# Taking GpSimd out of a weight conversion, norms off ScalarE, and a list schedule with other durations: windowed attention with a cosine-gated MLP on one core

## The chip, the cores and the metric

One core of a Trainium2 chip runs the kernel. The metric is the device time of one execution in microseconds (us). Engines are named as in the profile: PE is TensorE, DVE is VectorE, ACT is ScalarE, POOL is GpSimd, and SP is SyncE, which here only issues DMAs.

## The reference

```python
def _attn_ref(q, k, v, n_global, n_local):      # q, k, v: 4 x 8 x 768 x 64
    scores = scale * np.matmul(q, k.transpose(0, 1, 3, 2))
    ...                                          # is_global: the first 8 keys; is_local: the last 96
    scores = np.where(keep, scores + bias[None], -1000000000.0)
    a = np.exp(scores - np.max(scores, axis=-1, keepdims=True))
    a = a / (np.sum(a, axis=-1, keepdims=True) + 1e-09)
    return np.matmul(a, v).astype(np.float32)

def _moe_ref(x, w_in, w_out):                    # x: 3072 x 512, d_ff: 2048
    h = x @ w_in
    g = h * np.cos(h)
    return (g @ w_out).astype(np.float32)
```

The attention's output, 3072 tokens by 512, is the x of the second part. All numbers are 32-bit floats.

## The kernel before

The 3072 tokens are eight **chunks** of 384. A chunk has four head **pairs**, which gives 32 attention units. A unit's scores come from PE (L521 for the first eight units, L525 after), DVE folds and reduces them (L538, L547), ACT takes the exponentials (L572), DVE adds and inverts the sums (L580, L583), a **norm** multiplies the exponentials by the inverse, PE transposes them (L669), DVE masks them into `pv` (L677, L682), and PE multiplies by v (L704). The result is split into a high part `xh` and a rest `xl` (L725). Splitting every operand of a product into a rounded high part and a rest, and multiplying three times, is how 32-bit accuracy is kept.

The norm can run on three engines: one DVE instruction (L605, or two of L600 in a batch's first chunk), one or two POOL instructions of the same line, or four ACT instructions (L596).

The second part runs in 128 **steps**, one for each chunk and each of 16 slices f of d_ff. A step has 12 matmuls of 384 columns (L740, four quarters of three, one quarter for each pair of the chunk), then a chain over ACT and DVE (`turns` L757, `angle` L760, `cosine` L763, product L798, copy `gh`, difference `gl` L807), then 9 matmuls of 512 columns (L751). The steps are taken in phases: chunk 0 with slices 0 to 7, chunk 1 with all 16, chunk 0 with 8 to 15, then chunk by chunk. Steps are counted here from 0 in this order.

Weights arrive as 64-bit words and each of the 32 slices (`wi` and `wo`, 512 KB each) is **converted** on the chip by six instructions: `wlow` (L378 on ACT, L380 elsewhere), `wsign` (L385 on DVE, L388 on POOL), `wbias` (L394 on ACT, L396), `wjoin` (L399, DVE alone), `whigh` (L253 ACT, L255 DVE, L257 POOL) and `wrest` (L409).

A planner in the kernel decides the order. Each operation names its engines with a duration in ns on each, and what it must follow; `Plan.run` places them on a list schedule, earliest due first, and picks an engine by cost. The program is emitted in that order, so every engine runs its queue strictly in order. An operation with `port=True` is never planned at the same time on DVE as an instruction of POOL:

```python
                held = self.port > t
                holds = lambda o, x: x == POOL or (x == DVE and o.port)
...
                        if held and holds(o, e):
                            continue
```

`EARLY` spaces the due times of the four pairs of chunks 0 and 1. Where PE is planned to be idle in the first 45 us of the plan, filler matmuls on zeros (L1044) are emitted.

Of the kernel before, what the change touches and what calls it, by code (L numbers as in the profile page):

```python
# [27 lines left out]
SLOT = R + G  # L28
# [15 lines left out]
PERIOD = 5200  # L44
LAG = 3.5
MARGIN, EACH = 3.2, 3.2
EARLY = {0: 2500, 1: 7500}
WEIGHT = {PE: 1, ACT: 0.5, DVE: 1.2, POOL: 0.8}

PHASES = [(0, 0, 8), (1, 0, 16), (0, 8, 16)]  # L50
# [182 lines left out]
class Net:  # L233
# [124 lines left out]
    def plan_weights(self, f):  # L358


        nc, p = self.nc, self.plan
        cols = self.w_in.bitcast(U32)[f]
        rows = self.w_out.bitcast(U32)[f * P : (f + 1) * P, :]
        ends = []
        for kind, src, out in (("wi", cols, self.wi), ("wo", rows, self.wo)):
            raw = self.const.tile([P, 512, 2], U32, name="raw", tag=f"{kind}{f}")
            w0, w1 = raw[:, :, 0], raw[:, :, 1]
            wu = Slot("wu", lambda i: self.work.tile([P, 512], U32, name="wu", tag=i))
            box = {}

            def dma(e, raw=raw, src=src):
                nc.sync.dma_start(raw.rearrange("p c w -> p (c w)"), src)


            def wlow(e, raw=raw, w0=w0):
                h = raw.bitcast(I32)[:, :, 0]
                if e == ACT:
                    nc.scalar.activation(h, w0, AF.Copy, scale=7.49 * 2.0**-32)  # L378
                else:
                    self.eng(e).tensor_scalar(h, w0, 7.49 * 2.0**-32, 1.0, op0=ALU.mult, op1=ALU.mult)  # L380

            def wsign(e, raw=raw):
                if e == DVE:
                    h = raw.bitcast(U16)
                    nc.vector.tensor_scalar(h[:, :, 1], h[:, :, 3], 0x8000, None, op0=ALU.bitwise_and)  # L385
                else:
                    h = raw.bitcast(BF16)
                    nc.gpsimd.tensor_scalar(h[:, :, 1], h[:, :, 3], 0.0, 1.0, op0=ALU.mult, op1=ALU.mult)  # L388

            def wbias(e, w1=w1):  # L390

                x = w1.bitcast(F32)
                if e == ACT:
                    nc.scalar.activation(x, x, AF.Copy, scale=2.0**-112)  # L394
                else:
                    self.eng(e).tensor_scalar(x, x, 2.0**-112, 1.0, op0=ALU.mult, op1=ALU.mult)  # L396

            def wjoin(e, w0=w0, w1=w1, wu=wu):
                nc.vector.scalar_tensor_tensor(  # L399
                    wu.tile, w1, 3, w0, op0=ALU.logical_shift_left, op1=ALU.bitwise_or  # L400
                )

            def whigh(e, kind=kind, out=out, wu=wu, box=box):
                out[f] = box["w"] = self.const.tile([P, 2, 512], F32R, name="w", tag=f"{kind}{f}")
                self.copy(e, box["w"][:, 0, :], wu.tile.bitcast(F32))

            def wrest(e, wu=wu, box=box):
                w = box["w"]
                self.eng(e).tensor_tensor(  # L409
                    w[:, 1, :], wu.tile.bitcast(F32), w.bitcast(F32)[:, 0, :], op=ALU.subtract  # L410
                )

            o = p.op({SP: 470}, dma, extra=1460)
            o = p.op({ACT: 620, DVE: 400, POOL: 700}, wlow, [o], port=True)
            o = p.op({DVE: 610, POOL: 1310}, wsign, [o], port=True)
            o = p.op({ACT: 575, DVE: 345, POOL: 655}, wbias, [o], port=True)
            o = p.op({DVE: 605}, wjoin, [o], [wu], port=True)
            o = p.op({ACT: 525, DVE: 335, POOL: 595}, whigh, [o], [wu], port=True)
            ends.append(p.op({DVE: 605, POOL: 1245}, wrest, [o], [wu], port=True))
        return ends  # L420


# [41 lines left out]
    def plan_unit(self, L, pr):  # L464
# [13 lines left out]
        if exact:  # L478
            raw = row()
            src = self.qk[b, c, 2 * pr : 2 * pr + 2]  # L480

            def load(e):
                nc.sync.dma_start(raw.tile[:, k0:], src.rearrange("j p w -> (j p) w")[:, k0:])

            def queries(e):
                x = raw.tile[:, KW:]
                if e == ACT:
                    nc.scalar.activation(x, x, AF.Copy, scale=self.steep[:, pr : pr + 1])
                else:
                    self.eng(e).tensor_scalar(x, x, self.steep[:, pr : pr + 1], 1.0, op0=ALU.mult, op1=ALU.mult)  # L490

            o = p.op({SP: 470}, load, [], [raw], extra=1422 * (QK - k0) // 1000)
            ready = [p.op({ACT: 430, DVE: 270, POOL: 470}, queries, [o], [raw], port=True)]
            heads = [(raw, ready)] * 2
        else:
            heads = [self.plan_split(row(), self.qk[b, c, 2 * pr + j], k0, self.steepness(2 * pr + j)) for j in range(2)]
# [10 lines left out]
        for js, h in [(js, h) for js in (((0, 1),) if exact else ((0,), (1,))) for h in range(0, CT, 2)]:  # L507
# [17 lines left out]
                            nc.tensor.matmul(out, qs[:, m, q0], ks[:, k : k + w], start=m == 0, stop=m == 1)  # L525

            cols = sum(part(t)[1] for t in ts)
            cost = cols * 17 // 10 if exact else cols * 2 * 46 // 100
            so = self.chain("s", p.op(
                {PE: cost}, score, [o for j in js for o in heads[j][1]],  # L530
                list(pss.values()) + [heads[j][0] for j in js[:1]] + [st, tt[h // 2]], mode="rows" if exact else None,
# [1 line left out]
            for j, ps in pss.items():  # L533
                i0 = 1 if lead(h) else 0

                def fold(e, ps=ps, i0=i0):
                    w = ps.tile[:R, i0 * WIN : 2 * WIN].rearrange("p (a w) -> p a w", w=WIN)
                    nc.vector.copy_predicated(w[:, :, :R], self.mine.bitcast(U32)[:, i0:], w[:, :, SLOT:])  # L538

                o = p.op({DVE: 60 + 100 * (2 - i0)}, fold, [so], [ps])  # L540
                for i, t in enumerate(ts):

                    def least(e, i=i, t=t, j=j, ps=ps):
                        w = width(t)
# [37 lines left out]
        def rec(e):  # L582
            nc.vector.reciprocal(st.tile[:, 2 * n2 :], st.tile[:, n2 : 2 * n2])  # L583

        o = p.op({DVE: 70}, add, exps, [st])
        o = p.op({DVE: 120}, rec, [o], [st])
        u["norm"] = []
        for h in range(0, CT, 2):

            def norm(e, h=h):  # L590
                x = tt[h // 2].tile.rearrange("p t j w -> p (t j) w")
                r = st.tile[:, 2 * n2 + 2 * h : 2 * n2 + 2 * h + 4].rearrange("p (c o) -> p c o", o=1)
                if e == ACT:
                    for i in range(4):
                        w = width(h + i // 2)
                        nc.scalar.activation(x[:, i, :w], x[:, i, :w], AF.Copy, scale=r[:, i])  # L596
                    return
                if lead(h):
                    for a, w in ((0, R), (2, SLOT)):
                        self.eng(e).tensor_tensor(  # L600
                            x[:, a : a + 2, :w], x[:, a : a + 2, :w],
                            r[:, a : a + 2].broadcast_to([R, 2, w]), op=ALU.mult,
                        )
                    return
                self.eng(e).tensor_tensor(x, x, r.broadcast_to([R, 4, SLOT]), op=ALU.mult)  # L605

            u["norm"].append(
                p.op({DVE: 70 + 2 * 2 * SLOT * 104 // 100, ACT: 560, POOL: 100 + 4 * SLOT * 22 // 10}, norm, [o], [tt[h // 2], st], port=True)
            )
        return u  # L610

    def plan_split(self, raw, src, k0, sc):
# [27 lines left out]

        loads = [p.op({SP: 470}, lambda e, a=a: load(e, a), [], [raw], extra=711 * (QK - k0) // 1000) for a in (0, D)]
        w = KW - k0
        q = self.chain("qhigh", p.op({ACT: 370}, qhigh, loads, [raw, qk]))
        q = p.op({DVE: 470}, qrest, [q], [raw, qk], port=True)
        k = self.chain("khigh", p.op(
            {ACT: 50 + w * 427 // 512, DVE: 70 + w * 265 // 512, POOL: 100 + w * 490 // 512},
# [118 lines left out]
    def plan_step(self, s, n, f, a, b):  # L765
# [10 lines left out]
        for kk in range(self.NK):  # L776

            def m1(e, kk=kk):
                self.moe1(ph.tile, *x.tile, f, kk)

            done = self.chain(f"m1 {s}", p.op(
                {PE: 522}, m1, [self.xdone[n, kk], self.wdone[f][0]], [ph, x], due=due + (kk + 1) * 522,
            ))
            if kk == 0:
                self.chain("m1", done)
# [3 lines left out]
        for c0, c1 in pieces:  # L789
# [20 lines left out]
            for t in range(c0 // P, c1 // P):  # L810

                def m2(e, t=t):
                    self.moe2(po[t].tile, *gg.tile, f, t, f == a, f == b)

                o = self.chain("m2", p.op(
                    {PE: 697}, m2, [g, self.wdone[f][1]], [po[t], gg], due=due + int(LAG * PERIOD) + (t + 1) * 697,
                ))
                if f == b:
                    self.plan_store(n, t, po[t], o, b < self.NF - 1, due + int((LAG + 1) * PERIOD))
# [284 lines left out]
```

## Time and profile before

| what | value |
|---|---|
| median of 3 runs | 723.63 us (722.34 to 723.75) |
| the profiled execution's own time | 723.99 us |
| its span | 722.3 us |
| mean granted TensorE clock | 0.981 of full |
| PE, PEld busy | 697.8 us (97%), 603.4 us (84%) |
| DVE, ACT, POOL busy | 509.9 us (71%), 489.4 us (68%), 129.1 us (18%) |
| DMA | 55.75 MB, mean 77 GB/s |

Busy time is the time in which an engine had at least one instruction running; in a matmul row the modelled end is included, so neighbours overlap. 1.7 us of the execution's time lie outside the span. "Idle before" in a row is the idle time of that engine just ahead of the instruction, and the name behind the arrow is what ended it.

### The profile page before, as it was taken

How to read it: one execution, taken by the hardware profiler on the slowest of the kernel's cores; microseconds unless marked ns; L12 is line 12 of the kernel's file. 1: busy time of each engine (PE TensorE's matmuls, PEld its weight loads, DVE VectorE, ACT ScalarE, POOL GpSimd, SP SyncE). 2: the span in 40 equal slices, each digit the busy share in tenths (PEclk: the TensorE clock that was granted, in tenths of full speed). 3: DMA queues.
4: the chain of work that ended last, by engine and by line, in shares of the span. 5: the costliest groups of instructions: out<-in, count | busy, mean ns of one | idle time of the engine just before them, and what ended most of it. 6: DMA issues, size and time to landing. Idle time of an engine off the chain costs nothing.

```text
span 722.3 us, 13066 instructions
## 1 busy us (share of the span) xinstructions
PE 697.8 (97%) x4481; PEld 603.4 (84%) x4481; DVE 509.9 (71%) x1505; ACT 489.4 (68%) x1267; POOL 129.1 (18%) x170
## 2 busy tenths in 40 slices
PE   7977989999999999999999999999999999999996
PEld 4646768988899888888889888898888888989984
DVE  7898988886875887567774778757775778644332
ACT  7888987677775667577773886657775796644332
POOL 6345445630000211110000121101000120100000
PEclk8897999999999999999999999999999999999998
DMA  8997121022330322213121322203222210001001
GB/s 304 404 351 194 35 58 35 1 57 64 81 96 1 110 61 57 57 51 96 52 61 40 110 61 57 58 0 101 64 67 66 81 56 1 1 1 44 0 1 49
DMA packets 32605, 55.75 MB, mean 77 GB/s; under 512 B 3473, under 2 KB 18193, under 8 KB 32529
## 3 DMA queue, kind: packets, MB, share of 16 engines
q1 hardware_dynamic: 32528, 54.82, 25.4%
q8 instruction: 37, 0.61, 0.4%
q14 instruction: 40, 0.32, 0.1%
HBM read 48.52 MB, written 6.29 MB: 76 GB/s over the span
## 4 chain that ended last, share of the span: by engine, by line
PE 81%; DVE 7%; ACT 5%; issue 1%; DMA 0%; ACTq 0%; DVEq 0%
PE bank L740 34%; PE bank L751 34%; PE bank L704 5%; PE bank L525 5%; PE bank L669 3%; DVE wu L399 2%; DVE w L409 1%; ACT w L253 1%; ACT rr L763 1%; ACT raw L394 1%; DVE gl L807 1%; DVE tt L547 1%; ACT tt L596 1%; DVE bank L538 1%; DVE raw L385 1%
## 5 line engine op out<-in xcount | busy, mean ns | idle before, releaser
L740 PE MATMUL bank<-xh,w 128*128 128x384 f32 x1024 | 297.9, 343 | 4.4 <-DVE rr L798 3.2
L751 PE MATMUL bank<-w,gh 128*128 128x512 f32 x768 | 244.0, 399 | 0.0
L740 PEld LDWEIGHTS bank<-xh,w 128*128 128x128 f32 x1024 | 190.0, 190 | 12.0 <-DVE rr L798 3.6
L740 PE MATMUL bank<-xl,w 128*128 128x384 f32 x512 | 173.8, 339 | 2.7 <-DVE xl L725 2.7
L751 PEld LDWEIGHTS bank<-w,gh 128*128 128x128 f32 x768 | 138.9, 189 | 21.4 <-issue 0.3
L751 PE MATMUL bank<-w,gl 128*128 128x512 f32 x384 | 152.5, 397 | 0.0
L760 DVE SCALAR_TENSOR_TENSOR rr<-rr,bank 128x384 f32<-128x384 int32 x129 | 69.8, 543 | 104.4 <-ACT rr L757 104.3
L757 ACT ACTIVATE rr<-bank 128x384 int32<-128x384 f32 x129 | 62.0, 482 | 118.2 <-PE bank L740 117.8
L763 ACT ACTIVATE rr<-rr,half_pi 128x384 f32<-128x384 f32 x129 | 78.9, 614 | 43.9 <-DVE rr L760 42.7
L798 DVE TENSOR_TENSOR rr<-bank,rr 128x384 f32<-128x384 f32 x129 | 71.0, 552 | 46.7 <-ACT rr L763 45.9
L740 PEld LDWEIGHTS bank<-xl,w 128*128 128x128 f32 x512 | 97.3, 190 | 7.5 <-DVE xl L725 3.3
L572 ACT ACTIVATE tt<-tt,st 96x104 f32<-96x104 f32 (+1 forms) x256 | 94.4, 370 | 9.7 <-DVE st L547 8.2
L751 PEld LDWEIGHTS bank<-w,gl 128*128 128x128 f32 x384 | 72.4, 189 | 16.8
L257 POOL TENSOR_SCALAR ks<-raw 128x408 fp32r<-128x408 f32 (+1 forms) x43 | 24.7, 574 | 301.6 <-PE bank L525 284.3
L807 DVE TENSOR_TENSOR gl<-rr,gh 128x384 fp32r<-128x384 f32 (+1 forms) x115 | 66.7, 580 | 7.7 <-ACT gh L253 5.7
L547 DVE CUSTOM_DVE_ANT_0 tt<-bank,dd 96x104 f32<-96x104 f32 (+1 forms) x256 | 55.5, 257 | 3.0
L253 ACT CAST gh<-rr 128x384 fp32r<-128x384 f32 (+1 forms) x92 | 46.5, 507 | 11.3 <-DVE rr L798 4.6
L704 PEld LDWEIGHTS bank<-pv,v 104*64 104x64 f32 (+1 forms) x960 | 42.7, 140 | 12.8 <-issue 7.1
L596 ACT ACTIVATE tt<-tt,st 96x104 f32<-96x104 f32 (+1 forms) x152 | 44.6, 369 | 8.4 <-DVE st L583 8.1
L525 PEld LDWEIGHTS bank<-ks,qs 128*96 128x96 f32 x384 | 45.9, 162 | 4.7 <-issue 0.3
L704 PE MATMUL bank<-pv,v 104*64 104x96 f32 (+1 forms) x960 | 48.8, 254 | 0.6 <-ACT pv L253 0.6
L538 DVE COPY_PREDICATED bank<-mine,bank 96x192 f32<-96x192 uint32 (+1 forms) x128 | 40.6, 330 | 11.1 <-PE bank L525 8.0
(97 smaller groups left out, 766.5 us busy)
## 6 DMA issues: line engine op xcount, KB each, us to landing
raw<-in_qk_dram SPq DMA_DIRECT2D x48, 224.0 KB
raw<-in_qk_dram SPq DMA_DIRECT2D x48, 198.0 KB
raw<-in_w_in_dram SPq DMA_DIRECT2D x16, 512.0 KB
raw<-in_w_out_dram SPq DMA_DIRECT2D x16, 512.0 KB
out_dram<-oo SPq DMA_DIRECT2D x24, 256.0 KB
v<-in_v_dram SPq DMA_DIRECT2D x16, 240.0 KB
v<-in_v_dram SPq DMA_DIRECT2D x16, 192.0 KB
raw<-in_qk_dram SPq DMA_DIRECT2D x4, 448.0 KB
```

Of the source, the lines that this page charges most:

```text
L253: self.nc.scalar.copy(out, x)
L525: nc.tensor.matmul(out, qs[:, m, q0], ks[:, k : k + w], start=m == 0, stop=m == 1)
L547: nc.vector.tensor_tensor_reduce(tt[t // 2].tile[:, t % 2, j, :w], ps.tile[:R, i * WIN : i * WIN + w], self.dd[:, v, :w], op0=ALU.add, op1 ...
L572: nc.scalar.activation(x, x, AF.Exp, bias=st.tile[:, c : c + 1], scale=-1.0, accum_out=st.tile[:, n2 + c : n2 + c + 1])
L704: nc.tensor.matmul(px.tile[j * D : (j + 1) * D, t * R : (t + 1) * R], vs.tile[:k, t + c, hs][:, j * D : (j + 1) * D], pv[:k, c, o : o + R] ...
L740: self.nc.tensor.matmul(ph[:, :CW], self.wi[f][:, w, kk * P : (kk + 1) * P], xx[:, kk, :], start=kk == 0 and m == 0, stop=kk == self.NK - ...
L751: self.nc.tensor.matmul(po, gg[:, ts], self.wo[f][:, w, :], start=start and m == 0, stop=stop and m == 2)
L757: self.nc.scalar.activation(r.bitcast(I32), ph, AF.Copy, scale=1.0 / TWO_PI, bias=0.25)
L760: self.nc.vector.scalar_tensor_tensor(r, r.bitcast(I32), -TWO_PI, ph, op0=ALU.mult, op1=ALU.add)
L763: self.nc.scalar.activation(r, r, AF.Sin, bias=self.half_pi)
L798: {DVE: dve}, lambda e, r=r, h=h: nc.vector.tensor_tensor(r(), h(), r(), op=ALU.mult), [o], [ph, rr]
L807: self.eng(e).tensor_tensor(g[1][:, cs], r(), g[0].bitcast(F32)[:, cs], op=ALU.subtract)
```

## The change

The conversion's six operations lose their POOL durations, so that POOL has no part in it; the norm loses its ACT form; and a number of planned durations, the due spacing `EARLY`, and some `port` flags are other numbers. No arithmetic is added. The code that emits an instruction is the same apart from the norm's ACT branch.

```diff
-EARLY = {0: 2500, 1: 7500}
+EARLY = {0: 3000, 1: 6000}
...
             o = p.op({SP: 470}, dma, extra=1460)
-            o = p.op({ACT: 620, DVE: 400, POOL: 700}, wlow, [o], port=True)
-            o = p.op({DVE: 610, POOL: 1310}, wsign, [o], port=True)
-            o = p.op({ACT: 575, DVE: 345, POOL: 655}, wbias, [o], port=True)
-            o = p.op({DVE: 605}, wjoin, [o], [wu], port=True)
-            o = p.op({ACT: 525, DVE: 335, POOL: 595}, whigh, [o], [wu], port=True)
-            ends.append(p.op({DVE: 605, POOL: 1245}, wrest, [o], [wu], port=True))
+            o = p.op({ACT: 580, DVE: 500}, wlow, [o], port=True)
+            o = p.op({DVE: 650}, wsign, [o], port=True)
+            o = p.op({ACT: 580, DVE: 345}, wbias, [o], port=True)
+            o = p.op({DVE: 600}, wjoin, [o], [wu], port=True)
+            o = p.op({ACT: 525, DVE: 335}, whigh, [o], [wu], port=True)
+            ends.append(p.op({DVE: 600}, wrest, [o], [wu], port=True))
...
-            ready = [p.op({ACT: 430, DVE: 270, POOL: 470}, queries, [o], [raw], port=True)]
+            ready = [p.op({ACT: 520, DVE: 300, POOL: 490}, queries, [o], [raw], port=True)]
...
-        self.chain("worst", p.op({DVE: 75}, worst, [o for _, o in ttr], [st], due=self.xdue(n, pr)))
+        self.chain("worst", p.op({DVE: 80}, worst, [o for _, o in ttr], [st], due=self.xdue(n, pr), port=True))
...
-        o = p.op({DVE: 70}, add, exps, [st])
-        o = p.op({DVE: 120}, rec, [o], [st])
+        o = p.op({DVE: 85}, add, exps, [st], port=True)
+        o = p.op({DVE: 120}, rec, [o], [st], port=True)
...
-                if e == ACT:
-                    for i in range(4):
-                        w = width(h + i // 2)
-                        nc.scalar.activation(x[:, i, :w], x[:, i, :w], AF.Copy, scale=r[:, i])
-                    return
...
-                p.op({DVE: 70 + 2 * 2 * SLOT * 104 // 100, ACT: 560, POOL: 100 + 4 * SLOT * 22 // 10}, norm, [o], [tt[h // 2], st], port=True)
+                p.op({DVE: 70 + 4 * SLOT * 104 // 100, POOL: 850}, norm, [o], [tt[h // 2], st], port=True)
...
-        q = self.chain("qhigh", p.op({ACT: 370}, qhigh, loads, [raw, qk]))
+        q = self.chain("qhigh", p.op({ACT: 410}, qhigh, loads, [raw, qk]))
...
-                {PE: 522}, m1, [self.xdone[n, kk], self.wdone[f][0]], [ph, x], due=due + (kk + 1) * 522,
+                {PE: 527}, m1, [self.xdone[n, kk], self.wdone[f][0]], [ph, x], due=due + (kk + 1) * 527,
```

Four planned durations of fold, reduction, scores and the second matmuls change by 2 to 10 ns or 1% as well. In the changed kernel all lines from L596 on stand five lines higher, so its norm is L595 and L600, its `gl` L802, and its `xl` L720.

On POOL, behind its set-up (its last row is L315), this stood before: scaled queries (L490), and from there on mostly weights.

```order
L490 TENSOR_SCALAR raw<-raw,steep 128x384
L380 TENSOR_SCALAR raw<-raw 128x512
L388 TENSOR_SCALAR raw<-raw 128x512
L380 TENSOR_SCALAR raw<-raw 128x512 x2
L388 TENSOR_SCALAR raw<-raw 128x512
L396 TENSOR_SCALAR raw<-raw 128x512
L380 TENSOR_SCALAR raw<-raw 128x512
L490 TENSOR_SCALAR raw<-raw,steep 128x384
```

At the same place POOL's queue now holds queries, norms, and pieces of a step.

```order
L490 TENSOR_SCALAR raw<-raw,steep 128x384
L595 TENSOR_TENSOR tt<-tt,st 96x2x96
L595 TENSOR_TENSOR tt<-tt,st 96x208
L490 TENSOR_SCALAR raw<-raw,steep 128x384 x2
L600 TENSOR_TENSOR tt<-tt,st 96x416 x2
L257 TENSOR_SCALAR gh<-rr 128x384
L802 TENSOR_TENSOR gl<-rr,gh 128x384
```

All 56 weight instructions are gone from POOL. On DVE, at the end of the fourth unit's sums (L580, L583; one of its two norms was ACT's), stood before:

```order
L580 TENSOR_SCALAR st<-st 96x8
L583 RECIPROCAL st<-st 96x8
L399 SCALAR_TENSOR_TENSOR wu<-raw 128x512
L605 TENSOR_TENSOR tt<-tt,st 96x416
L563 TENSOR_TENSOR worst<-worst,st 96x8
L399 SCALAR_TENSOR_TENSOR wu<-raw 128x512
L409 TENSOR_TENSOR w<-wu,w 128x512
```

The same place of DVE's queue in the changed kernel, with the `wsign` of the next weights (L385) behind it:

```order
L580 TENSOR_SCALAR st<-st 96x8
L583 RECIPROCAL st<-st 96x8
L399 SCALAR_TENSOR_TENSOR wu<-raw 128x512
L595 TENSOR_TENSOR tt<-tt,st 96x2x96
L595 TENSOR_TENSOR tt<-tt,st 96x208
L600 TENSOR_TENSOR tt<-tt,st 96x416
L409 TENSOR_TENSOR w<-wu,w 128x512
L672 TENSOR_TENSOR pv<-bank,others 104x192
L720 TENSOR_TENSOR xl<-bank,xh 128x384
L672 TENSOR_TENSOR pv<-bank,others 104x384
L677 TENSOR_TENSOR pv<-bank,own 96x384
```

Both norms and the sign instructions have moved onto DVE here. On SP, the DMA of chunk 1's third pair stood before between weights:

```order
L372 DMA raw<-in_w_in_dram 128x1024
L372 DMA raw<-in_w_out_dram 128x1024
L483 DMA raw<-in_qk_dram 128x896
L372 DMA raw<-in_w_in_dram 128x1024
L372 DMA raw<-in_w_out_dram 128x1024
L438 DMA v<-in_v_dram 96x5x128
```

Now it stands five weights and one v load later:

```order
L372 DMA raw<-in_w_in_dram 128x1024
L438 DMA v<-in_v_dram 96x5x128
L441 DMA v<-in_v_dram 8x4x128
L483 DMA raw<-in_qk_dram 128x896
L372 DMA raw<-in_w_out_dram 128x1024 x4
```

## Rows read from the trace of the kernel before

**Rows 1.** By stretch: its length, busy us of five engines, clock, DMA, GB/s.

```profile
20.00:110.00 90.00, 77.82 (x560) 57.59 (x558) 82.14 (x226) 78.47 (x212) 40.55 (x39) 0.91 0.61 202
111.00:180.00 69.00, 68.04 (x403) 60.29 (x403) 55.57 (x129) 50.82 (x118) 26.46 (x22) 1.00 0.14 38
180.00:640.00 460.00, 460.00 (x3044) 408.22 (x3043) 326.38 (x1002) 314.22 (x818) 49.95 (x68) 1.00 0.21 58
```

**Rows 2.** Waits of PE from 111 to 700 us: total, times, longest.

```profile
PE bank L669 <- ACT tt L596: 0.9, 1, 0.9
```

**Rows 3.** Timeline of PE: start, us, instruction, idle before.

```profile
76.42 0.92 PE L521 MATMUL bank<-raw 64*96 64x200 f32 x8
...
101.62 1.11 PE L669 MATMUL bank<-ident,tt 96*104 96x96 f32 x4 [2.48 <-ACT tt L596]
...
110.55 0.44 PE L740 MATMUL bank<-xl,w 128*128 128x384 f32 x1 [0.32 <-DVE xl L725]
...
179.93 0.62 PE L751 MATMUL bank<-w,gh 128*128 128x512 f32 x2
```

**Rows 4.** DVE from 20 to 110 us by line and shape: busy us, mean ns.

```profile
L399 DVE SCALAR_TENSOR_TENSOR wu<-raw 128x512 uint32<-128x512 uint32 x19 | 14.9, 797 | 0.0
L409 DVE TENSOR_TENSOR w<-wu,w 128x512 fp32r<-128x512 f32 x17 | 14.1, 831 | 0.3 <-ACT w L253 0.3
L807 DVE TENSOR_TENSOR gl<-rr,gh 128x384 fp32r<-128x384 f32 x8 | 5.7, 706 | 1.6 <-ACT gh L253 1.6
L385 DVE TENSOR_SCALAR raw<-raw 128x512 uint16<-128x512 uint16 x5 | 4.8, 959 | 0.0
L798 DVE TENSOR_TENSOR rr<-bank,rr 128x384 f32<-128x384 f32 x8 | 4.4, 557 | 2.0 <-ACT rr L763 1.9
L580 DVE TENSOR_SCALAR st<-st 96x8 f32<-96x8 f32 x6 | 2.5, 417 | 0.1
L255 DVE CAST w<-wu 128x512 fp32r<-128x512 f32 x1 | 1.6, 1552 | 0.0
```

**Rows 5.** The same view of DVE from 300 to 640 us.

```profile
L798 DVE TENSOR_TENSOR rr<-bank,rr 128x384 f32<-128x384 f32 x65 | 36.0, 554 | 21.5 <-ACT rr L763 21.3
L807 DVE TENSOR_TENSOR gl<-rr,gh 128x384 fp32r<-128x384 f32 x57 | 31.4, 551 | 1.5 <-ACT gh L253 0.5
L580 DVE TENSOR_SCALAR st<-st 96x8 f32<-96x8 f32 x16 | 2.6, 165 | 0.2
```

**Rows 6.** Timeline of DVE where its instructions follow each other.

```profile
33.94 0.68 DVE L409 TENSOR_TENSOR w<-wu,w 128x512 fp32r<-128x512 f32 x1
34.55 1.28 DVE L399 SCALAR_TENSOR_TENSOR wu<-raw 128x512 uint32<-128x512 uint32 x2
35.75 0.25 DVE L547 CUSTOM_DVE_ANT_0 tt<-bank,dd 96x104 f32<-96x104 f32 x1
...
36.49 0.73 DVE L385 TENSOR_SCALAR raw<-raw 128x512 uint16<-128x512 uint16 x1
37.02 0.71 DVE L409 TENSOR_TENSOR w<-wu,w 128x512 fp32r<-128x512 f32 x1
```

**Rows 7.** Timeline of POOL at 123.6 us and of DVE beside it.

```profile
123.64 1.67 POOL L388 TENSOR_SCALAR raw<-raw 128x512 bf16<-128x512 bf16 x1
...
124.01 1.56 DVE L399 SCALAR_TENSOR_TENSOR wu<-raw 128x512 uint32<-128x512 uint32 x1
```

**Rows 8.** Groups of ACT over the whole span: busy us, mean ns.

```profile
L596 ACT ACTIVATE tt<-tt,st 96x104 f32<-96x104 f32 (+1 forms) x152 | 44.6, 369 | 8.4 <-DVE st L583 8.1 <-ACT oo L253 0.3
L378 ACT ACTIVATE raw<-raw 128x512 int32<-128x512 uint32 x23 | 14.9, 672 | 0.0
```

**Rows 9.** The chain of work that ended last, two pieces of the closed run.

```profile
204.18 2.11 PE bank L740 x12
...
235.22 2.09 PE bank L751 x9
```

**Rows 10.** The page's GB/s, 40 slices of 18 us.

```profile
GB/s 304 404 351 194 35 58 35 1 57 64 81 96 1 110 61 57 57 51 96 52 61 40 110 61 57 58 0 101 64 67 66 81 56 1 1 1 44 0 1 49
```

More of the change, by code (lines that the diff above doesn't have):

```diff
@@ L527, in plan_unit @@
             cols = sum(part(t)[1] for t in ts)
-            cost = cols * 17 // 10 if exact else cols * 2 * 46 // 100
+            cost = cols * 17 // 10 if exact else cols * 2 * 47 // 100
             so = self.chain("s", p.op(
@@ L538, in fold @@
                     nc.vector.copy_predicated(w[:, :, :R], self.mine.bitcast(U32)[:, i0:], w[:, :, SLOT:])
-                o = p.op({DVE: 60 + 100 * (2 - i0)}, fold, [so], [ps])
+                o = p.op({DVE: 70 + 98 * (2 - i0)}, fold, [so], [ps])
                 for i, t in enumerate(ts):
@@ L556, in least @@
                         )
-                    ttr.append(((t, j), p.op({DVE: 180}, least, [o, self.masked], [ps, tt[t // 2], st])))
+                    ttr.append(((t, j), p.op({DVE: 188}, least, [o, self.masked], [ps, tt[t // 2], st])))
         n2 = 2 * CT
@@ L815, in plan_step @@
                 o = self.chain("m2", p.op(
-                    {PE: 697}, m2, [g, self.wdone[f][1]], [po[t], gg], due=due + int(LAG * PERIOD) + (t + 1) * 697,
+                    {PE: 700}, m2, [g, self.wdone[f][1]], [po[t], gg], due=due + int(LAG * PERIOD) + (t + 1) * 697,
                 ))
```

## The prediction

> **What bounds the kernel now.** I read the busy time by stretch first, then PE's waits, then DVE by line and shape in two stretches, then the timelines of DVE and POOL side by side. The stretches [rows 1] split the run in two. From 180 to 640 us PE is busy without a gap at clock 1.00, while DVE is busy 326 of 460 us; there nothing on DVE, ACT or POOL can change the time. From 20 to 110 us PE is busy 77.8 of 90 us at a mean clock of 0.91, and part of that is filler matmuls; there DVE is busy 82.1 us and ACT 78.5 us: DVE is the fullest engine that does only real work. Between 111 and 700 us PE waits once, for 0.9 us [rows 2].
>
> So the time is set by when PE gets into its closed run. I take as **point A** the matmul that first uses the last `xl` of chunk 1: it starts at 110.55 us, released by that `xl` [rows 3]. Ten us earlier PE stood 2.48 us for a norm on ACT [rows 3], the last of the same unit. Whatever moves A forward, with the same work behind it, comes off the time one for one, as long as PE isn't starved afterwards.
>
> Why is DVE so full before A? The same shapes last longer there than later. `gl` takes 706 ns from 20 to 110 us and 551 ns from 300 to 640, the small addition L580 417 against 165 [rows 4, 5]. The product L798, one of whose inputs lies in PSUM, takes 557 against 554, no difference [rows 4, 5]. POOL is busy 40.6 us of those 90, against 50 of 460 later [rows 1]. And where they meet it can be seen singly: while POOL's `wsign` runs 1.67 us, DVE's `wjoin` holds its queue for 1.56 us [rows 7]; elsewhere two of them take 1.28 together and start 0.60 apart [rows 6].
>
> The Trainium skill ("SBUF — State Buffer", Who interferes with whom) says that DVE and GpSimd share one pair of SBUF ports under an exclusive lock, so that the later instruction blocks for the whole of the other, and that a DVE instruction with at most one SBUF input outside the two-port modes does not contend. L798 against `gl` agrees. Taken at its most, by the rule all 40.6 us of POOL could be lost to DVE, and A would come that much sooner; the rows bear out a quarter of it, which is what I sum by.
>
> **The change, part by part.** *Weights off POOL: the stretch.* Count times excess over the unhindered duration. The unhindered `wjoin` is 1.28 - 0.60 = 0.68, `wrest` 0.68 and `wsign` at most 0.73 [rows 6]. `wjoin` 19 x (0.797 - 0.68) = 2.2 us, `wrest` 17 x (0.831 - 0.68) = 2.6, `gl` 8 x 0.155 = 1.2, `wsign` 5 x 0.23 = 1.2, L580 6 x 0.25 = 1.5 (part of it may be a wait), the one copy of a weight 1.55 - 0.73 = 0.8 [rows 4 to 6]: 9.5 us, say 10 of the 90 with what is too small for the rows. POOL keeps some work in the changed order. Ahead of A its queue holds 5 scaled queries, 4 whole norms and 2 halves, 2 `gh`, 2 `gl` and 2 splits of keys, about 13 us where it had 40.6; at the same ratio 3 us of stretch stay.
>
> *Weights off POOL: the work.* It must be done by others. Priced start to start (`wsign` 37.02 - 36.49 = 0.53, `wrest` 34.55 - 33.94 = 0.61, `wjoin` 0.60 [rows 6]; others the mean less 0.08, the overlap seen there), DVE's queue ahead of the last `xl` of chunk 1 adds up to the same in both orders, some 79 us. The changed order has 10 `wsign` more (+5.3), 3 whole and 6 half norms more (about +3.2) and 3 more copies of weights (+1.0), but 5 `wjoin` and 3 `wrest` fewer (-4.8), 2 products, 1 `angle` and 4 `gl` fewer (-3.3; two of those `gl` are on POOL), and no rest of queries, one bias and one copy less (-1.5). So A is reached with the same DVE work, but with 14 weights joined instead of 19: what is gained there is partly owed later.
>
> *Norms off ACT.* Ahead of the last exponential of chunk 1, ACT loses 36 instructions L596, 0.37 less 0.08 each [rows 8], 10.4 us, and the wait of 2.48 us at 101.62 loses its cause; it gains 7 `wlow` and 3 `wbias`, at 0.67 less 0.08 each [rows 8] about 6 us, and loses 3 scalings, 3 `whigh`, 2 `cosine` and 2 `gh`, about 5. ACT has some 9 us less to do there, so it does not take DVE's place.
>
> *`EARLY` and the queue of DMAs.* SP's order moves chunk 0's fourth pair behind one more weight and chunk 1's third pair behind five weights and a v load. At the 350 to 404 GB/s of the first 54 us [rows 10] a weight of 512 KB takes 1.3 to 1.5 us, so the latter lands 7 to 9 us later. It costs nothing while that pair's scores, at 76.42 us [rows 3], still come after the traffic falls to 35 GB/s at 72 us [rows 10]; without that cover it would cost at most those 9 us.
>
> *Sum at A.* 110.55 - 10 + 3 = 103.5 us by the stretch alone. The waits, 7.9 us of idle DVE from 20 to 110 [rows 1], I let stand, except for the norm of 2.48 us and about 1 us more, as ACT is lighter: A at 100.0. The bounds are 97 (L580's excess and the instructions too small for the rows, 4 us more) and 107 (ACT and the DMA hold what POOL has let go).
>
> *Work of PE behind A.* Both orders have the same matmuls ahead of A, but the changed one 6 fewer of L751: at 2.09 / 9 = 0.23 us each [rows 9] 1.4 us are owed later. From A to the end of the execution before are 723.99 - 110.55 = 613.4 us. 100.0 + 613.4 + 1.4 = 714.8.
>
> *Stage B, from A until DVE has done `gl` of step 20*, which takes in all remaining conversions. In the order before, A to the second product of that step took PE 179.93 - 110.55 = 69.4 us [rows 3]; the changed order has 0.7 us less there (12 fewer of L740, 2.1, and 6 more of L751, 1.4 [rows 9]): 68.7. DVE must do 18 `wjoin` (10.8), 17 `wsign` (9.0), 18 `wrest` (11.0), 42 instructions of steps at 0.47 (19.7) and the attention of two units with splits (about 13.5): 64 us, where the order before had 42, the rest being POOL's or done already. If DVE works 90 of 100 us, as it nearly did from 20 to 110 (82.1 of 90, with stretch now small), that is 71.1, and PE waits 71.1 - 68.7 = 2.4 us. At 0.93 it is nothing, at 0.86 5.7. I take 1.7, since part of DVE's idling falls where PE has work queued: **716.5 us**, 1% under the execution's own 723.99 and under the median of 723.63, which lies only 0.4 lower. The likeliest case alone spans 712 to 721.
>
> **The rivals.** *VectorE becomes the bound of stage B, and the kernel ends slower.* For it speaks that DVE has 64 us of work where PE has 68.7, after a stage in which it was never free. The gain at A, 10.55 - 1.4 = 9.2 us, is lost when DVE needs 77.9 us, a working share of 0.82. From 20 to 110 us the 79 us of priced work less the 11 before 20 us were 68 of 90, 0.76, but with 10 us of stretch that mostly goes. At 0.76 stage B lasts 84.2 us, 15.5 more than PE wants: 714.8 + 15.5 = 730. It ends slower, beyond 725.4, below a share of 0.81. Against it: ACT's queue is lighter in stage B, so DVE waits less for it. The Trainium skill ("Perfetto Trace Analysis", Optimizing Scalar/DVE Operations) advises, where DVE is saturated, to move work to Scalar or even GpSimd, which is this change undone; the same section doubts it between DVE and GpSimd because of the shared port.
>
> *A hardly moves.* DVE's instructions are shorter, but their inputs come no sooner: weights are still landing at 194 GB/s between 54 and 72 us [rows 10], and ACT is busy 78.5 of 90 us [rows 1]. Then A stays at about 105 to 107, and with nothing owed in stage B the time is 720 to 722. ACT's 9 us less speak against it.
>
> *Better than the sum.* A at 97, and no wait in stage B: 97 + 613.4 + 1.4 = 711.8; the stretch in 111 to 180 us hid behind PE and gives nothing. Below 708 the rows offer no source except waits that I let stand.
>
> **How the numbers follow.** The likeliest (A at 98 to 103, a small loss in B, 712 to 721) has 0.58; A hardly moved 0.14; better, under 712, 0.09; VectorE as the bound 0.19, of it 0.08 about even and 0.11 slower. A measurement here tells 0.2%, 1.45 us, from no change, so the borders are 722.2 and 725.1. A tenth of the "hardly moved" case falls among no change. The range of 708 to 724 leaves out the slower case and a little below.
>
> **What would show it.** Right: `wjoin` and `wrest` near 0.68 us and `gl` near 0.55 before 100 us, no L388 on POOL; the first use of chunk 1's last `xl` at 97 to 103 us; PE closed from then on but for a few waits for `gl` up to step 20. Wrong: PE waits of several us in total for DVE between 100 and 170 us (the first rival), or A later than 105 us with DVE idle for ACT or DMA (the second). The clock matters little: its mean is 0.91 up to 110 us and 1.00 behind it [rows 1], and the steps ahead of A have room.

## The result, and the profile after

| version | median us | range | ratio to before, 95% interval |
|---|---|---|---|
| before | 723.39 | 722.34 to 723.75 | 1 |
| after | 715.23 | 711.82 to 716.25 | 0.9882 (0.9852 to 0.9911) |

8.2 us faster by the medians; forecast were 716.5 us, 708 to 724. (The median of before is here over four executions; the prediction had three.) The profiled execution of after took 711.82 us (span 710.0). It is its fastest, 3.4 us under the median: its mean granted clock was 0.993, that of four others, which took 714.8 to 716.3 us, 0.981 to 0.988. So between the two profiles there are 12.2 us to explain, where the medians differ by 8.2. In after, lines from L596 on have numbers five smaller, so L669 is L664 there.

The same three stretches as in [rows 1], with the same columns:

```profile
20.00:110.00 90.00, 82.44 (x582) 64.35 (x579) 87.62 (x256) 80.15 (x195) 14.57 (x16) 0.96 0.62 204
111.00:180.00 69.00, 67.70 (x417) 60.44 (x417) 64.35 (x178) 52.12 (x127) 5.75 (x9) 1.00 0.12 32
180.00:640.00 460.00, 457.40 (x3038) 407.57 (x3037) 328.93 (x999) 281.38 (x708) 50.62 (x62) 1.00 0.23 58
```

POOL fell from 40.55 to 14.57 us in the first stretch, and DVE is now busy 87.62 of 90 us. From 111 to 180 us DVE is busy 0.93 of the time, and PE still nearly all of it. PE's waits from 111 to 700 us, to be held against [rows 2]:

```profile
PE bank L664 <- DVE tt L600: 1.9, 5, 1.0
PE bank L664 <- POOL tt L600: 0.7, 3, 0.3
PE bank L699 <- DVE pv L677: 0.4, 1, 0.4
PE bank L699 <- DMA raw<-in_qk_dram: 0.4, 1, 0.4
PE bank L664 <- ACT oo L253: 0.3, 1, 0.3
```

None is for `gl`. Norms, now on DVE and POOL, stop PE eight times for 2.6 us in all, where before had one wait of 0.9 us. DVE by line and shape from 20 to 110 us, as in [rows 4]:

```profile
L385 DVE TENSOR_SCALAR raw<-raw 128x512 uint16<-128x512 uint16 x21 | 15.7, 766 | 0.0
L409 DVE TENSOR_TENSOR w<-wu,w 128x512 fp32r<-128x512 f32 x19 | 13.9, 737 | 0.7 <-ACT w L253 0.6
L399 DVE SCALAR_TENSOR_TENSOR wu<-raw 128x512 uint32<-128x512 uint32 x19 | 13.1, 694 | 0.0
L793 DVE TENSOR_TENSOR rr<-bank,rr 128x384 f32<-128x384 f32 x11 | 6.1, 555 | 0.6 <-ACT rr L758 0.6
L802 DVE TENSOR_TENSOR gl<-rr,gh 128x384 fp32r<-128x384 f32 x8 | 4.5, 558 | 0.3 <-issue 0.3
L600 DVE TENSOR_TENSOR tt<-tt,st 96x416 f32<-96x416 f32 x6 | 4.3, 728 | 0.0
L580 DVE TENSOR_SCALAR st<-st 96x8 f32<-96x8 f32 x6 | 1.1, 188 | 0.0
```

`wjoin` 797 to 694 ns, `wrest` 831 to 737, `wsign` 959 to 766, `gl` 706 to 558, the addition 417 to 188; the product L793, which reads one input from PSUM, stayed (557, 555). The timeline of PE, to be held against [rows 3]:

```profile
83.96 1.55 PE L699 MATMUL bank<-pv,v 104*64 104x96 f32 x32
87.10 0.84 PE L664 MATMUL bank<-ident,tt 96*104 96x96 f32 x8 [1.59 <-DVE tt L600]
88.53 2.84 PE L699 MATMUL bank<-pv,v 104*64 104x96 f32 x32 [0.59 <-DVE pv L672]
...
96.53 0.34 PE L735 MATMUL bank<-xl,w 128*128 128x384 f32 x1
...
166.37 0.63 PE L746 MATMUL bank<-w,gh 128*128 128x512 f32 x2
```

From 88.5 us on PE runs closed but for the waits above. Point A is at 96.53 us, without a wait; step 20's second product (L746, before L751) begins at 166.37 us where it began at 179.93. DVE's part is best seen up to the start of chunk 1's last `xl`. Busy time of before up to it, then of after:

```profile
0.00:109.95 109.95, 93.94 (x664) 67.70 (x664) 96.63 (x310) 93.23 (x271) 52.73 (x80) 0.89 0.67 222
```

```profile
0.00:92.34 92.34, 78.73 (x623) 56.94 (x624) 86.61 (x313) 81.31 (x227) 20.77 (x52) 0.96 0.77 259
```

That `xl` starts 17.6 us earlier: DVE's busy time ahead of it (third busy figure) fell by 10.0 us, with three instructions more, and its idle time by 7.6 (13.3 to 5.7).

### The profile page after: what moved, and what is told of

Its sections match the earlier page's. It is cut to its first block, busy times and chain, and to the rows that moved or that the text cites. A ratio compares the mean times of both kernels' runs of the same rounds, so it can differ in the third digit from the quotient of the medians.

```text
span 710.0 us, 12912 instructions
## 1 busy us (share of the span) xinstructions
PE 684.9 (96%) x4477; PEld 597.2 (84%) x4477; DVE 523.3 (74%) x1575; ACT 455.7 (64%) x1139; POOL 77.8 (11%) x124
## 4 chain that ended last, share of the span: by engine, by line
PE 74%; DVE 13%; DMA 6%; ACT 5%; issue 1%; SPq 1%; POOL 0%; ACTq 0%; POOLq 0%; DVEq 0%
PE bank L735 32%; PE bank L746 31%; PE bank L699 5%; PE bank L525 3%; DMA raw<-in_w_out_dram 3%; PE bank L664 2%; DMA raw<-in_w_in_dram 2%; ACT tt L572 2%; DVE tt L547 2%; DVE rr L755 1%; DVE bank L538 1%; DVE w L409 1%; DVE wu L399 1%; ACT L572 1%; DVE raw L385 1%
## 5 line engine op out<-in xcount | busy, mean ns | idle before, releaser
L735 PE MATMUL bank<-xh,w 128*128 128x384 f32 x1024 | 297.2, 343 | 0.9 <-DVE rr L793 0.6
L746 PE MATMUL bank<-w,gh 128*128 128x512 f32 x768 | 243.5, 398 | 0.0
L735 PEld LDWEIGHTS bank<-xh,w 128*128 128x128 f32 x1024 | 189.2, 189 | 8.5 <-DVE rr L793 1.0
L735 PE MATMUL bank<-xl,w 128*128 128x384 f32 x512 | 173.2, 338 | 0.0
L746 PEld LDWEIGHTS bank<-w,gh 128*128 128x128 f32 x768 | 138.4, 188 | 21.6 <-issue 0.5
L746 PE MATMUL bank<-w,gl 128*128 128x512 f32 x384 | 152.0, 396 | 0.0
L735 PEld LDWEIGHTS bank<-xl,w 128*128 128x128 f32 x512 | 97.2, 190 | 4.0
L572 ACT ACTIVATE tt<-tt,st 96x104 f32<-96x104 f32 (+1 forms) x256 | 94.2, 370 | 4.8 <-DVE st L547 4.2
L793 DVE TENSOR_TENSOR rr<-bank,rr 128x384 f32<-128x384 f32 x129 | 70.6, 551 | 35.7 <-ACT rr L758 35.3
L746 PEld LDWEIGHTS bank<-w,gl 128*128 128x128 f32 x384 | 72.1, 188 | 16.7
L253 ACT CAST gh<-rr 128x384 fp32r<-128x384 f32 (+1 forms) x100 | 50.8, 509 | 30.7 <-DVE rr L793 21.9
L802 DVE TENSOR_TENSOR gl<-rr,gh 128x384 fp32r<-128x384 f32 (+1 forms) x114 | 62.7, 550 | 7.9 <-ACT gh L253 5.4
L257 POOL TENSOR_SCALAR ks<-raw 128x408 fp32r<-128x408 f32 (+1 forms) x38 | 22.7, 597 | 333.0 <-PE bank L525 293.0
L699 PEld LDWEIGHTS bank<-pv,v 104*64 104x64 f32 (+1 forms) x960 | 42.1, 138 | 14.1 <-issue 8.2
L699 PE MATMUL bank<-pv,v 104*64 104x96 f32 (+1 forms) x960 | 48.9, 252 | 2.7 <-DVE pv L672 1.8
L572 ACT ACTIVATION_READ_ACCUMULATOR tt<-tt,st 96x1 f32 x256 | 48.1, 188 | 0.0
L525 PE MATMUL bank<-ks,qs 128*96 128x200 f32 (+1 forms) x384 | 47.7, 255 | 0.0
```

The lines of the kernel that those rows point to most:

```text
L253: self.nc.scalar.copy(out, x)
L572: nc.scalar.activation(x, x, AF.Exp, bias=st.tile[:, c : c + 1], scale=-1.0, accum_out=st.tile[:, n2 + c : n2 + c + 1])
L699: nc.tensor.matmul(px.tile[j * D : (j + 1) * D, t * R : (t + 1) * R], vs.tile[:k, t + c, hs][:, j * D : (j + 1) * D], pv[:k, c, o : o + R] ...
L735: self.nc.tensor.matmul(ph[:, :CW], self.wi[f][:, w, kk * P : (kk + 1) * P], xx[:, kk, :], start=kk == 0 and m == 0, stop=kk == self.NK - ...
L746: self.nc.tensor.matmul(po, gg[:, ts], self.wo[f][:, w, :], start=start and m == 0, stop=stop and m == 2)
L793: {DVE: dve}, lambda e, r=r, h=h: nc.vector.tensor_tensor(r(), h(), r(), op=ALU.mult), [o], [ph, rr]
```

## The experiments

Three theories were there before the first run: **S**, the gain is DVE no longer stretched by POOL, that is, its instructions no longer last longer beside POOL's; **W**, it is PE no longer waiting for norms on ACT; **N**, it is the other numbers, which re-order the opening. The change has three parts: the weights off POOL, the norm off ACT, and the numbers (durations, `EARLY`, port flags). The first eight lines of this table are all their combinations; two more theories, M and L, came up behind them (e10 to e13). The ratio of a run is to executions of before taken beside it, whose median was 722.7 to 723.4 us.

| run | POOL converts | norm on ACT | numbers | median us | ratio, 95% interval |
|---|---|---|---|---|---|
| before | yes | yes | old | 723.39 | 1 |
| e3 | yes | yes | new | 720.84 | 0.9978 (0.9965 to 0.9991) |
| e2 | yes | no | old | 718.91 | 0.9941 (0.9926 to 0.9956) |
| e1 | no | yes | old | 714.54 | 0.9881 (0.9862 to 0.9900) |
| e8 | yes | no | new | 712.59 | 0.9853 (0.9835 to 0.9870) |
| e7 | no | yes | new | 711.49 | 0.9844 (0.9825 to 0.9864) |
| e5 | no | no | old | 713.10 | 0.9864 (0.9840 to 0.9888) |
| after | no | no | new | 715.23 | 0.9882 (0.9852 to 0.9911) |
| e10, before + 5 ns | yes | yes | old | 718.50 | 0.9938 (0.9926 to 0.9951) |
| e12, e1 + 5 ns | no | yes | old | 715.16 | 0.9892 (0.9875 to 0.9909) |
| e13, e8 + 5 ns | yes | no | new | 718.62 | 0.9935 (0.9919 to 0.9950) |
| e11, after + 5 ns | no | no | new | 708.91 | 0.9816 (0.9798 to 0.9833) |
| e9, after + 1 idle addition | no | no | new | 719.82 | 0.9957 (0.9940 to 0.9973) |
| e4, after + 4 | no | no | new | 762.99 | 1.0547 (1.0526 to 1.0567) |

**e1, the weights alone.** Of the diff only this, in all six operations:

```diff
-            o = p.op({DVE: 610, POOL: 1310}, wsign, [o], port=True)
+            o = p.op({DVE: 610}, wsign, [o], port=True)
```

> The kernel before with one part of the change: the six conversion operations lose their POOL durations, everything else (ACT norm, old durations, old EARLY) stays. Theory S (the gain comes from DVE no longer being stretched by POOL): 7 of the 12 us between the two profiles come from here, so 717 to 720 us, wjoin and wrest near 0.70 us before 100 us. Rival N (the other numbers, which re-order the opening, made the gain): 722 us or more, however short DVE's instructions get. Rival W (waits for ACT's norms made it): 721 or more, with PE still standing for L596.

714.54 us: this part alone gives the whole gain, 2.5 us below the lowest time that S gave. W and N, as the only cause, fall with it: both had 721 us or more. Its stretch from 20 to 110 us and PE's timeline there:

```profile
20.00:110.00 90.00, 84.29 (x590) 62.99 (x589) 84.06 (x250) 87.18 (x240) 11.45 (x11) 0.94 0.60 198
```

```profile
95.61 1.30 PE L669 MATMUL bank<-ident,tt 96*104 96x96 f32 x8
...
102.82 0.42 PE L740 MATMUL bank<-xl,w 128*128 128x384 f32 x1
```

In before PE had stood 2.48 us, at 101.62 us [rows 3], for the norms of one unit. In e1 it takes up the same norms at 95.61 us without a wait, though ACT is fuller than before (87.18 us) and has more norms, and A is at 102.82 us. ACT's norms in this stretch, of before and then of e1 (instructions, busy us, mean ns, idle time just ahead of them and what ended it):

```profile
L596 ACT ACTIVATE tt<-tt,st 96x104 f32<-96x104 f32 (+1 forms) x32 | 9.3, 370 | 4.7 <-DVE st L583 4.7
```

```profile
L596 ACT ACTIVATE tt<-tt,st 96x104 f32<-96x104 f32 (+1 forms) x44 | 12.7, 372 | 0.6 <-DVE st L583 0.6
```

In before, ACT itself had stood 4.7 us for the reciprocal on DVE (L583); in e1, 0.6 us. For the wait at 101.62 us the trace of before shows the whole chain, POOL, DVE and ACT:

```profile
96.90 3.14 POOL L388 TENSOR_SCALAR raw<-raw 128x512 bf16<-128x512 bf16 x2
```

```profile
97.28 1.56 DVE L409 TENSOR_TENSOR w<-wu,w 128x512 fp32r<-128x512 f32 x1
98.77 1.55 DVE L255 CAST w<-wu 128x512 fp32r<-128x512 f32 x1
```

```profile
101.19 2.29 ACT L596 ACTIVATE tt<-tt,st 96x104 f32<-96x104 f32 x8 [1.81 <-DVE st L583]
```

Beside two `wsign` of POOL, a `wrest` and a copy of a weight hold DVE's queue for 3 us (unhindered a `wrest` takes 0.68 us [rows 6], such a copy 0.41 in the mean of after), the reciprocal behind them ends at 101.09, and ACT has stood 1.81 us for it. The wait that bore ACT's name was DVE's lateness, passed on, and DVE's was the stretch.

One sign of S failed. `wrest` and `wsign` came down to 682 and 751 ns, but `wjoin`, expected near 0.70 us, stayed as it was (797 in before):

```profile
L399 DVE SCALAR_TENSOR_TENSOR wu<-raw 128x512 uint32<-128x512 uint32 x19 | 14.9, 789 | 0.3 <-ACT raw L394 0.2
```

Singly, 15 of these 19 took 0.68 to 0.72 us and four 0.91 to 1.54, each of the four beside one of POOL's few instructions; in before 15 took 0.64 to 0.69 and four 1.13 to 1.55, again each beside POOL. So the stretch is a matter of which instructions meet, and POOL's busy time prices it on average only. And as e1 has another order too, it doesn't show by itself that all of its gain is stretch.

**e2 and e3, the two other parts alone.** e2 takes `ACT: 560` out of the old norm; e3 is the changed kernel with POOL's old durations and the ACT form put back.

> The kernel before with another part: the norm loses its ACT form, POOL keeps its conversions. Theory S: 2.5 to 3.5 us at most, 720 to 722 us, and not below, as DVE and POOL get the norms and DVE is already full. Rival W: 717 or less. The norms go to DVE or POOL, so a loss (725 or more) would say that DVE's fill counts for more than ACT's wait.

> The changed kernel with POOL's old durations put back into the conversion and the ACT form put back into the norm: only EARLY, the port flags and the re-told durations of the change are left. Theory S: 721 us or more, since POOL converts again. Rival N: 717 or less.

718.91 and 720.84 us: by the ratios the norm gave 4.3 us, the numbers 1.6. Neither theory had the norm's time: it is under the 720 of S and over the 717 of W. N, which had 717 or less for the numbers, falls.

**e5, e7 and e8, two parts of the three.** e5 is e1 with `ACT: 560` out of the norm as well; e7 puts `ACT: 560` and its four instructions back into the changed norm; e8 puts the POOL durations of before back into the changed conversion.

> The kernel before with two parts of the change, weights off POOL and norm off ACT, and none of the numbers. If the two gains measured alone (8 us and 4 us) come from different time, they add: 710 to 712 us. If both remove the same time (the late start of PE's closed run, which the norms' waits only pass on), they don't: 713 to 716 us. The prediction's sum had 7 us for the first and 3.5 for the second and added them.

> The changed kernel with the ACT form put back into the norm: weights off POOL and the numbers. By the prediction's sum the ACT form costs 3.5 us here: 718 to 720 us. If the weights alone carry the gain: 714 to 716.5 us, as the changed kernel.

> The changed kernel with POOL's old durations put back into the conversion: norm off ACT and the numbers are left. Theory S (POOL's weights are the cost): 718 to 721 us, with wjoin, wrest and wsign at 0.75 to 0.95 us before 110 us. If the norm and the numbers were enough: 717 or less.

The medians of all three lie below the changed kernel, though the intervals overlap. Beside the weights, the norm gains nothing that can be told (e5 against e1; the executions of e5 lie at 710.8 to 715.5 us). e7 lies below both of its forecasts. And e8 goes against S: POOL converts as much as ever. Its first stretch, DVE's norm in it, and POOL's `wsign`:

```profile
20.00:110.00 90.00, 81.57 (x600) 64.25 (x598) 85.60 (x238) 77.47 (x194) 51.62 (x45) 0.94 0.61 203
```

```profile
L600 DVE TENSOR_TENSOR tt<-tt,st 96x416 f32<-96x416 f32 x9 | 10.0, 1136 | 0.0
```

```profile
L388 POOL TENSOR_SCALAR raw<-raw 128x512 bf16<-128x512 bf16 x18 | 27.7, 1589 | 0.6 <-ACT raw L378 0.3
```

The stretch is there (a norm lasts 1136 ns where it lasts 728 in after), but the 18 `wsign` on POOL also spare DVE 18 x 0.53 = 9.5 us, by the price of the prediction. So what e8 tells is that POOL's conversions cost and spare at once.

**e4 and e9, POOL work that nobody waits for, in after's own order.** This is the test of the stretch with no instruction moved. Behind each weight's `wrest`, POOL adds the finished weight's halves into a spare tile that nothing reads, four times (e4) or once (e9); line numbers behind it are four larger than in after, those of `wsign` to `wrest` one:

```diff
+                for i in (0,):              # e4: (0, 0, 256, 256)
+                    x = w.bitcast(F32)[:, :, i : i + 256]
+                    nc.gpsimd.tensor_tensor(self.spare, x[:, 0], x[:, 1], op=ALU.add)
```

> The changed kernel in its own order, with four POOL additions of 128x256 behind each of the 32 weights' wrest, which read the finished weight and write a spare tile that nobody reads or waits for: some 35 us more of POOL ahead of point A, nothing more on any other engine, no order changed. Theory S: at the quarter that the prediction took, DVE loses 9 us ahead of A; 5 to 9 us over the changed kernel, 720 to 724 us, with wjoin, wrest and wsign back at 0.75 to 0.95 us. If stretch plays no part in the gain (rivals N and W): within 1.5 us of the changed kernel, 714 to 717.

> As the run with four idle additions behind each weight, with one: some 10 us more of POOL ahead of point A, 32 x 0.65 to 1.0 us in all, which hardly delays POOL's own queue. Theory S at the quarter of the prediction: 2 to 4 us over the changed kernel, 717 to 719 us. If the 48 us of the run with four came from POOL's queue (norms and gl behind the additions) and not from DVE's stretch: within 1.5 us, 714 to 716.7.

e9, 719.82 us, 4.6 over the changed kernel, and the ratios' intervals lie apart. POOL's additions and DVE from 20 to 110 us:

```profile
L415 POOL TENSOR_TENSOR spare<-w 128x256 f32<-128x256 f32 x17 | 16.7, 980 | 52.6 <-DVE w L410 49.7 <-DVE st L584 1.7 <-ACT raw L379 1.1
```

```profile
L386 DVE TENSOR_SCALAR raw<-raw 128x512 uint16<-128x512 uint16 x18 | 14.0, 811 | 0.0
L400 DVE SCALAR_TENSOR_TENSOR wu<-raw 128x512 uint32<-128x512 uint32 x18 | 13.3, 743 | 0.0
L410 DVE TENSOR_TENSOR w<-wu,w 128x512 fp32r<-128x512 f32 x17 | 12.3, 728 | 1.3 <-ACT w L253 1.1
L604 DVE TENSOR_TENSOR tt<-tt,st 96x416 f32<-96x416 f32 x6 | 5.6, 944 | 0.0
L797 DVE TENSOR_TENSOR rr<-bank,rr 128x384 f32<-128x384 f32 x9 | 5.0, 554 | 1.7 <-ACT rr L762 1.7
L806 DVE TENSOR_TENSOR gl<-rr,gh 128x384 fp32r<-128x384 f32 x6 | 4.8, 802 | 0.3 <-issue 0.3
L584 DVE TENSOR_SCALAR st<-st 96x8 f32<-96x8 f32 x6 | 1.5, 256 | 0.0
```

Against after: norms 6 x 0.216, `gl` 6 x 0.244, `wsign` 18 x 0.045, `wjoin` 18 x 0.049, additions 6 x 0.068, `wrest` 17 x -0.009: 4.7 us of DVE for 16.7 of POOL, 0.28 per us. The product from PSUM took 554 ns. POOL's own queue is not the cause: from 20 us on PE waits for POOL 0.7 us in all, as in after, and from 20 to 110 us DVE and ACT never do. PE's last large waits of the opening, which after has at 87.10 and 88.53 us, come 5.1 us later:

```profile
92.18 0.84 PE L668 MATMUL bank<-ident,tt 96*104 96x96 f32 x8 [1.57 <-DVE tt L604]
93.62 2.97 PE L703 MATMUL bank<-pv,v 104*64 104x96 f32 x32 [0.59 <-DVE pv L676]
```

The two profiled executions lie 9.6 us apart (721.46 and 711.82): A is 6.6 us later (103.13), and 3.3 more are lost from there to step 20's second product, where PE waits longer for DVE than in after.

e4 was missed widely: 48 us where I had expected 5 to 9. Of PE's waits from 20 to 700 us:

```profile
PE bank L668 <- DVE tt L599: 8.9, 2, 4.6
PE bank L668 <- DVE tt L604: 6.7, 7, 3.9
...
PE bank L750 <- POOL gl L806: 3.9, 1, 3.9
PE bank L668 <- POOL tt L604: 3.7, 4, 3.1
```

I had priced DVE's stretch alone. POOL's own `gl` and norms also stand behind the additions in its queue, and PE waits for them, and for DVE, which waited in turn (7.7 us for `gh` on POOL from 20 to 200 us). How the 48 us divide between queue and stretch isn't settled. What e4 shows singly is the stretch itself. DVE and POOL at the same place:

```profile
63.78 0.55 DVE L797 TENSOR_TENSOR rr<-bank,rr 128x384 f32<-128x384 f32 x1
...
65.64 0.95 DVE L567 TENSOR_TENSOR worst<-worst,st 96x8 f32<-96x8 f32 x1
```

```profile
61.81 3.14 POOL L415 TENSOR_TENSOR spare<-w 128x256 f32<-128x256 f32 x4
...
65.51 1.05 POOL L806 TENSOR_TENSOR gl<-rr,gh 128x384 fp32r<-128x384 f32 x1
```

A maximum over eight columns, which starts 0.13 us behind POOL's `gl`, lasts until `gl` ends (66.59 and 66.56 us); the product from PSUM, amid POOL's additions, isn't touched. In after such a maximum takes 0.11 us (at 85.06 us). The Trainium skill ("SBUF — State Buffer", Who interferes with whom) says that a DVE instruction with two SBUF inputs contends with a GpSimd instruction that reads SBUF, under an exclusive lock, and one with at most one such input, outside its two-port modes, does not; the trace agrees here: the maximum, with two, took 0.95 us for 0.11, and the product, with one, 0.55 as elsewhere.

**e10 to e13, the same plan told 5 ns more.** That three versions with a part left out lie below the whole left the question how much of 2 to 4 us is a part's price (theory M) and how much is the order in which the list schedule happens to fall (theory L).

```diff
-            o = p.op({DVE: 605}, wjoin, [o], [wu], port=True)      # e10 (before) and e12 (e1)
+            o = p.op({DVE: 610}, wjoin, [o], [wu], port=True)
-            o = p.op({DVE: 650}, wsign, [o], port=True)            # e11 (after); in e13 (e8) beside POOL
+            o = p.op({DVE: 655}, wsign, [o], port=True)
```

> The kernel before with one planned duration 5 ns longer (wjoin 605 to 610), which means nothing for the engines but re-orders DVE's queue (381 lines of difference) and POOL's. Theory M (each part of the change has its own price): within 1.5 us of the kernel before, 721.5 to 725. Theory L (a good part of the differences of 2 to 4 us between the versions is how one order happens to fall): it moves by 2 us or more, to either side.

> The changed kernel with one planned duration 5 ns longer (wsign 650 to 655), which re-orders its queues as well. Theory M: 714 to 716.5 us. Theory L: 2 us or more away, most likely down, as the three versions with one part left out lie at 711.5 to 713.

> The kernel before with only the weights taken off POOL and wjoin 5 ns longer in the plan. Theory M: 713 to 716 us, as without the 5 ns. Theory L: 2 us or more away. In both the gain over the kernel before should stay at 5 us or more, if POOL's stretch is its cause.

> The changed kernel with POOL's durations back in the conversion and wsign 5 ns longer in the plan. Theory M: 711 to 714 us, below the changed kernel, which would say that POOL's conversions pay for their stretch once the norms are off ACT. Theory L: 2 us or more above, level with the changed kernel or over it, which would say that its 712.6 us was one lucky order.

They moved by -4.5 us (723.0 beside it), -6.3 (-4.8 by the ratios), +0.6 and +6.0. Three of four moved as L said; e12 stayed, as M said, and kept its gain over before. The 712.59 of e8 was the better of two orders, and the changed kernel is not the best order of its own plan either: with 5 ns more in its plan it takes 708.91 us, the fastest of all and below both kernels. There DVE is busy 89.39 of 90 us:

```profile
20.00:110.00 90.00, 83.51 (x606) 64.26 (x607) 89.39 (x261) 85.37 (x209) 12.13 (x13) 1.00 0.63 208
```

Much of the 5 ns shows up at A, the first matmul with chunk 1's last `xl`. In e10, e8 and e13:

```profile
104.24 0.64 PE L740 MATMUL bank<-xl,w 128*128 128x384 f32 x1 [2.58 <-DVE xl L725]
```

```profile
99.71 0.34 PE L735 MATMUL bank<-xl,w 128*128 128x384 f32 x1
```

```profile
106.15 0.44 PE L735 MATMUL bank<-xl,w 128*128 128x384 f32 x1 [0.67 <-DVE xl L720]
```

A moved by -6.3 us from before to e10, by +6.4 from e8 to e13, by -1.4 from after to e11 (95.17). In e12 it came 5.3 us sooner than in e1 (97.52), but with 3.0 us more of matmuls owed behind it. In the twelve orders A moves over 15 us, and A, the matmuls owed and the 613.4 us of the prediction give the profiled execution's time within 3.3 us. So what an order is worth is mostly how soon it reaches A and what it owes then; why one order is there sooner than another is open.

Taken as groups, the six orders in which POOL converts (before, e2, e3, e8, e10, e13) lie at 712.6 to 723.4, 718.8 in the mean; the six in which it doesn't (e1, e5, e7, e11, e12, after) at 708.9 to 715.2, 713.1 in the mean. 5.7 us are the weights' part in the mean, though the groups overlap. The same mean over the norm is 717.3 with and 714.6 without the ACT form, and over the numbers 717.3 old and 714.6 new: 2.7 us each, less than the orders scatter.

## Why the prediction was right

**The number** held (716.5, measured 715.23), and the mechanism held in its main line: POOL's work stretched DVE, DVE set the time of A, and A the time of the kernel. Point by point it held less well, and that the number is within 1.3 us is in part luck.

- *DVE full and stretched by POOL.* Right, and shown with the order fixed by e9: 0.28 us of DVE per us of POOL, where the prediction took 10 of 40.6, 0.25. In after the durations came down towards those listed there.
- *The same DVE work, 10 us of stretch off, 3 back.* 7 us of busy time; measured 10.0. Right in kind, 3 us short.
- *Waits 2.5 + 1, as ACT is lighter.* Mis-sized and wrongly attributed. DVE idled 7.6 us less, and by e1 the wait at 101.62 us goes without touching a norm: its cause stood two links back, in POOL's `wsign`. Taking norms off ACT gains nothing beside the weights that could be told (e5, e7). I had let the idle time stand.
- *A at 100.0, bounds 97 and 107.* Measured 96.53, just outside. (The lower bound counts L580's excess again, which the 9.5 us hold already.) The last `xl` was ready at 92.9 us, so A had ceased to be the gate; the norm at 87.10 and the `pv` at 88.53 us were the last to stop PE, both DVE's.
- *The same matmuls ahead of A but for 6 of L751.* This step failed: counted in PE's queue, before has 115 of L740 ahead of A, after 106 of L735. Nine at 2.11 / 12 us [rows 9], 1.6 us, are owed besides the 1.4.
- *Stage B, 1.7 us.* Nothing measurable: from A to step 20's second product 69.8 us, where the 68.7 with the nine matmuls put right make 70.3. DVE worked 0.93 of the time (I had 0.90), PE waited twice for a norm, 1.2 us, and never for `gl`.

So the sum closes otherwise than forecast: A -14.0, owed +3.0, and 1.1 less behind A (0.4 up to step 20's product and 0.7 after it, not followed further): -12.1 of the 12.2 us between the profiles. The terms' errors, -3.5 at A, +1.6, -1.7 and -1.1, add to -4.7, the distance from 716.5 to the profile's 711.82. That the median is nearer is luck, as the sum was for the profiled execution. Of the rivals, VectorE as the bound and A hardly moved didn't occur; the profile itself sits on *better than the sum* (A at 97, no wait, 711.8), the median in the likeliest case.

*`EARLY` and the DMAs* cost nothing visible: no wait of PE from 0 to 111 us ended with a DMA. The chain of after does run over four landing weights from 5.1 to 40.2 us. But that is no floor: the chain of e11, which is faster, runs over ACT and DVE there and over no weight. `EARLY` by itself wasn't tried.

What the argument lacked altogether is L. It read one order against one other order and gave the parts prices of 1 to 3 us, when 5 ns in the plan move the kernel by up to 6. Of its terms, 3.5 us went to the norms, which gain nothing beside the weights, and 1.7 us to a loss in stage B that did not come, and the sum still came out near. The range of 16 us was wide enough for that by other reasons.

## What to carry to other kernels

Where a list schedule sets the order, time each version in several orders (a few ns on one planned duration make one) before a part of a change gets a price; the best order may be worth more than half of the change (e11). By e9, as an estimate, the price of moving work from POOL to a full DVE is its duration on DVE less about 0.3 of its duration on POOL, so look at what it costs on each: 0.53 against 1.6 us for `wsign` is near even, and e8 and e13 fall on both sides of after. The 5.7 us between the groups don't follow from this estimate; it matters which instruction is hit and what waits behind it. A wait's releaser names the last link, not the cause: before an engine is relieved because another waits for it, ask what that engine was waiting for.

## What the hardware showed unexpectedly

An instruction of DVE on eight columns can last nearly as long as a POOL instruction of 1.05 us (0.95 us in e4, where it takes 0.11 alone; the small addition has a mean of 0.417 us from 20 to 110 us in before, against 0.165 later). So small instructions suffer most for their size.

And the clock took its share at the same place. In after, 32 matmuls of L699 took 1.55 us at 83.96 us and 32 of the same shape 2.84 us at 88.53 us. The granted clock (third figure from the end) was full from 84 to 88 us and at its lower level, 0.5, from 89.3 to 92.5:

```profile
84.00:88.00 4.00, 2.35 (x41) 1.99 (x40) 3.93 (x10) 3.97 (x8) 1.20 (x1) 1.00 0.18 54
89.30:92.50 3.20, 3.20 (x30) 2.98 (x29) 3.20 (x8) 1.60 (x4) 0.00 (x0) 0.50 0.01 3
```

Just before 88.53 us, PE had stood 1.59 and 0.59 us. But in e11 it stood 1.95 us at 51.65 us, and the clock stayed at 1.00 from 20 to 110 us; so what brings it down isn't shown here.
